# A recurrent attention with a squared-ReLU MLP: new engine orders, half-size operations in the first two steps

## Chip, cores, metric

One core of a Trainium2 chip. The time is device microseconds of one execution, the median of several runs; lower is better. "Span" is the time from the first to the last instruction in the profiled execution.

## What is computed

Four batches, eight heads, 768 positions, 48 channels a head. A decayed outer-product state runs along the positions; its readings, laid side by side over the heads (384 columns), go through a two-layer MLP with a squared ReLU.

```python
# r, k, v, w: (4, 8, 768, 48) f32; u: (8, 48)
for t in range(S):
    cur = einsum('bhd,bhe->bhde', u[None] * kt, vt)
    y[:, :, t] = einsum('bhd,bhde->bhe', rt, state + cur)
    state = wt[:, :, :, None] * state + einsum('bhd,bhe->bhde', kt, vt)
x = y.transpose(0, 2, 1, 3).reshape(3072, 384)
h = x @ w_in                      # w_in (384, 2048)
out = maximum(h, 0) ** 2 @ w_out  # w_out (2048, 384), out (3072, 384) f32
```

## The kernel before

The 3072 rows are cut into 12 **steps** of 256 positions (three a batch). A step lies on 128 partitions, two neighbouring positions (j) a partition, and consists of two chunks (c) of 128 positions. The words below are the names of the operations; `x.s` is the operation x of step s.

*Attention of a step.* `ld.s.w/r/k/v` load 384 KB each through the DMA queue of SP. `ww`, `lw` multiply neighbouring decays and take the log; `cum` sums the logs by matmuls into the PSUM pair `att`; `exp` and `ac` turn the sums into decays. `rw`, `kw` scale one neighbour of r and of k; `rd.s.0` (r) and `rd.s.1` (k) multiply by the decays into `rdec`. These are transposed, by TensorE (`tr`, copied out by `rkt`) in steps 0 to 2 and by DMA (`dtr`) from step 3. `p` multiplies k against r, `pm` masks the product, `su` sums k against v, `ts` and `sn` carry the state S to the next chunk. `ku`, `qp`, `q`, `vq` make the share of u. `y`, `yq`, `yc` add three products up in one PSUM pair, `ysb` copies them out as bf16, `yt` and `xt` (steps 0 to 3) or `dyt` (DMA, later steps) transpose them to `xT`.

*MLP of a step.* Eight `m1.s.g` (six matmuls each) make 2048 hidden columns; `rl.s.g` applies the ReLU and `sq.s.q` squares two groups. In steps 0 to 4 `m2.s.c.q` (four matmuls) multiplies by w_out, and `os` scales. In steps 5 to 11 seven products of halves (`pw.s.1` to `.7`) with sums of halves (`sw`, `tw`) take the place of the eight, put together by `cx` and `ow`. `store` writes 128 rows. w_in and w_out come in four loads each (`ld.g.i`, `ld.g.o`, 768 KB, staging buffers `w_st`) and are cast to f16 (`cast.i.g`, `cast.o.g`). m1 groups 0 and 1 need cast.i.0, 2 and 3 cast.i.1, 4 and 5 cast.i.2, 6 and 7 cast.i.3.

*Order.* The string ORDER is the program: its words are issued one after the other, and each engine works off its own words strictly in this order, waiting for what a word needs. `=A`, `=V`, `=G` put a word on ScalarE (ACT), VectorE (DVE) or GpSimd (POOL); `:n` names the PSUM bank (`one[0..3]`, or pair `att[0..1]`; m, n are pairs of single banks). So the order on an engine and the choice of engine are both written in this string. `warm_.n.i` issues n matmuls on zeros.

*Buffers* go round in lists: `buf(kind, key)` counts the uses of a buffer, given in advance, and puts it back after the last. A load into a buffer waits on SP until it is free, and everything behind it on SP waits too.

Of the kernel before, what the change touches and what calls it, by code (L numbers as in the profile page):

```python
# [22 lines left out]
pm_.1.1 cast.i.1=A yt_.0:3 sn_.0.1 su_.1:0 xt_.0=V qp_.1 ts_.1.0=V m1_.0.1:3 cast.i.2=A pm_.1.0 m1_.0.3:2 m1_.0.0:0  # L23
rl_.0.1=A sn_.1.0 q_.1 ld.2.v cast.i.3=A m1_.0.2:1 rl_.0.3=V m1_.0.4:3 vq_.1 ld.0.o ts_.1.1=V rl_.0.2=A y_.1:1
rl_.0.0=V yc_.1 ld.3.k ww_.2=G yq_.1 m1_.0.5:2 ysb_.1=V ku_.2 m1_.0.6:0 lw_.2 rl_.0.4=V rl_.0.5=A yt_.1:1 sq_.0.0=A
cum_.2:1 ld.1.o xt_.1=V m1_.0.7:3 ld.3.w kw_.2=G rl_.0.6=A m1_.1.1:1 ld.2.o exp_.2 sn_.1.1 m1_.1.4:2 rl_.1.1=V
rl_.0.7=A m1_.1.0:0 rw_.2=G sq_.0.3=A rl_.1.4=V m1_.1.5:1 rl_.1.0=V qp_.2 m1_.1.7:2 rd_.2.0 rl_.1.5=A m1_.1.6:0 ld.3.r
rl_.1.7=A rd_.2.1 tr_.2.0:3 cast.o.0=G rl_.1.6=A m1_.1.2:1 ld.3.o rkt_.2.0=V v_.2=A tr_.2.1:2 rl_.1.2=A m1_.1.3:0
ku_.3 rkt_.2.1=V ac_.2 sq_.1.0=A su_.2:0 q_.2 m2_.0.0.0:1 ld.4.w m2_.0.1.0:3 ts_.2.0=V sq_.0.1=A cast.o.1=G rl_.1.3=V
ld.3.v p_.2.0:1 p_.2.1:0 ww_.3=V sq_.1.1=A m2_.1.1.0:0 vq_.2 m2_.1.0.0:2 pm_.2.1 lw_.3 sq_.1.2=A m2_.0.0.1 pm_.2.0  # L30
# [649 lines left out]
```

## Time and profile before

| | |
|---|---|
| time, median of 3 runs | 178.31 us (177.84 to 179.43) |
| span of the profiled execution | 176.7 us (its whole time is not given; the median lies 1.6 us above the span) |
| PE (matmul) busy | 168.7 us, 95% of the span |
| DVE, ACT, POOL busy | 141.4, 135.7, 125.8 us |
| HBM read, written | 25.17 MB, 4.72 MB |

Busy times are sums over one engine; PE is the matmul row of TensorE, PEld its weight loads, which lie beside it. In a list of instructions the columns are start, duration, engine, source line, operation, output and inputs, shapes, count, and in brackets the idle time before it with what ended that time. Matmul durations include the way through the array, so groups of few matmuls look longer than the distance to the next group. L517 is m1, L540 m2, L594 pw, L454 the y products, L408 p, L430 su, L383 tr, L500 yt, L336 to L340 cum, L238 the spreading of u, L622 the warm-ups.

### The profile page before, as it was taken

The numbers are of one execution on the slowest core, as the hardware profiler recorded it, in microseconds if no ns is written. First come the engines' busy times: TensorE is split into PE (matmuls) and PEld (weight loads), VectorE is DVE, ScalarE is ACT, GpSimd is POOL, SyncE is SP. The second block draws the span as 40 slices with busy tenths as digits, with TensorE's granted clock in tenths as the row PEclk, the third lists the DMA queues.
The fourth block names the chain that finished last, engine by engine and source line by source line (L and its number), as shares of the span: only waits on it lengthen the run. The fifth ranks groups of instructions, "written<-read, shape, count | busy, mean of one in ns | idle before, by whom it ended". The sixth has DMA issues, their size and how long they took to land.

```text
span 176.7 us, 5829 instructions
## 1 busy us (share of the span) xinstructions
PE 168.7 (95%) x2431; PEld 133.3 (75%) x2431; DVE 141.4 (80%) x221; ACT 135.7 (77%) x229; POOL 125.8 (71%) x116
## 2 busy tenths in 40 slices
PE   7969799999999999999999999999999999999993
PEld 2336678866687677578776888889988888989992
DVE  5299976994888968997877979979899879788731
ACT  5677799998659896939899799997897688477320
POOL 6298979999978099969999319759939665165220
DMA  5999999999699999797999959989959930330123
GB/s 142 315 305 340 380 244 347 370 347 254 152 220 240 287 199 254 184 215 179 308 225 194 329 136 222 224 113 269 251 115 132 227 53 4 108 114 4 45 93 134
DMA packets 82667, 36.55 MB, mean 207 GB/s; under 512 B 75857, under 2 KB 81106, under 8 KB 82642
## 3 DMA queue, kind: packets, MB, share of 16 engines
q1 hardware_dynamic: 82642, 36.19, 82.7%
q8 instruction: 19, 0.31, 0.7%
q14 instruction: 6, 0.05, 0.1%
HBM read 25.17 MB, written 4.72 MB: 169 GB/s over the span
## 4 chain that ended last, share of the span: by engine, by line
PE 85%; SPq 6%; DMA 5%; issue 1%; ACT 1%; ACTq 0%
PE one L517 35%; PE one L594 19%; PE one L540 15%; PE att L454 7%; DMA w_st_b<-in_moe_w_in_dram 5%; SPq L205 4%; PE att L408 3%; PE att L430 2%; SPq L213 2%; PE att L338 1%; SPq L233 1%; PE one L500 1%; PE att L340 1%; PE one L383 1%; PE att L336 0%
## 5 line engine op out<-in xcount | busy, mean ns | idle before, releaser
L517 PE MATMUL one<-xT_b,wi_sb 128*128 128x256 bf16 x576 | 70.3, 273 | 0.6 <-ACT gt_b L524 0.4
L517 PEld LDWEIGHTS <-wi_sb 128*128 128x128 f16 x576 | 54.7, 98 | 9.4 <-issue 1.3
L524 ACT ACTIVATE gt_b<-one 128x512 f16<-128x512 f32 x70 | 40.8, 596 | 10.1 <-PE one L517 9.4
L532 ACT ACTIVATE gt_b<-gt_b 128x1024 bf16<-128x1024 f16 x42 | 43.5, 1056 | 1.4 <-DVE gt_b L526 1.0
L419 DVE TENSOR_TENSOR pmT_b<-att,mask 128x1024 bf16<-128x1024 f32 x22 | 26.3, 1217 | 4.2 <-PE att L408 4.2
L540 PE MATMUL one<-wo_sb,gt_b 128*128 128x384 f16 x160 | 28.7, 326 | 0.0
L594 PEld LDWEIGHTS <-gt_b 128*128 128x128 bf16 x280 | 23.2, 98 | 0.9 <-issue 0.4
L311 POOL TENSOR_TENSOR ku_b<-k_b,u_bc 128x768 f32<-128x768 f32 x12 | 22.3, 1862 | 1.0 <-ACT ac_buf L360 0.8
L316 POOL TENSOR_TENSOR ku_b<-ku_b,r_b 128x768 f32<-128x768 f32 x12 | 22.2, 1848 | 0.6 <-DMA r_b<-in_r_dram 0.4
L540 PEld LDWEIGHTS <-gt_b 128*128 128x128 bf16 x160 | 15.1, 98 | 9.6 <-issue 0.5
L444 POOL TENSOR_TENSOR S_b<-t_b,ac_buf 128x384 bf16<-128x384 f32 x20 | 16.9, 846 | 5.4 <-ACT t_b L438 4.8
L526 DVE TENSOR_SCALAR gt_b<-one 128x512 f16<-128x512 f32 x26 | 17.6, 686 | 3.0 <-PE one L517 2.2
L322 POOL TENSOR_TENSOR vq_b<-v_b,q_b 128x768 bf16<-128x768 f32 x12 | 18.2, 1518 | 0.9 <-DVE q_b L319 0.8
L594 PE MATMUL one<-wo_sb,gt_b 128*128 128x192 f16 x168 | 16.2, 246 | 0.0
L374 DVE TENSOR_TENSOR rdec_buf<-r_b,att 128x768 bf16<-128x768 f32 x12 | 11.4, 948 | 1.8 <-POOL r_b L304 0.8
L374 DVE TENSOR_TENSOR rdec_buf<-k_b,att 128x768 bf16<-128x768 f32 x12 | 11.4, 948 | 1.7 <-ACT ac_buf L360 1.1
L319 DVE TENSOR_REDUCE q_b<-ku_b 128x16 f32<-128x768 f32 x12 | 11.3, 944 | 1.7 <-POOL ku_b L316 1.7
L599 ACT ACTIVATE w_st_b<-one 128x192 f32<-128x192 f32 x14 | 4.4, 329 | 10.3 <-PE one L594 10.2
L304 POOL TENSOR_TENSOR r_b<-r_b,w_b 128x384 f32<-128x384 f32 x8 | 8.1, 1014 | 4.7 <-DMA r_b<-in_r_dram 4.7
L292 POOL TENSOR_TENSOR ww_b<-w_b 128x384 f32<-128x384 f32 x7 | 8.0, 1149 | 4.5 <-DMA w_b<-in_w_dram 4.5
L594 PE MATMUL one<-w_st_b,gt_b 128*128 128x192 f16 x112 | 11.2, 246 | 0.0
L440 DVE TENSOR_TENSOR t_b<-S_b,att 128x384 f32<-128x384 bf16 x16 | 8.8, 548 | 2.9 <-POOL S_b L444 2.8
(100 smaller groups left out, 266.5 us busy)
## 6 DMA issues: line engine op xcount, KB each, us to landing
w_b<-in_w_dram SPq DMA_DIRECT2D x12, 384.0 KB, 5.9
r_b<-in_r_dram SPq DMA_DIRECT2D x12, 384.0 KB, 5.4
k_b<-in_k_dram SPq DMA_DIRECT2D x12, 384.0 KB, 5.3
v_b<-in_v_dram SPq DMA_DIRECT2D x12, 384.0 KB, 5.0
out_dram<-w_st_b SPq DMA_DIRECT2D x23, 192.0 KB, 2.2
w_st_b<-in_moe_w_in_dram SPq DMA_DIRECT2D x4, 768.0 KB, 9.5
w_st_b<-in_moe_w_out_dram SPq DMA_DIRECT2D x4, 768.0 KB, 9.1
rkT_b<-rdec_buf SPq DMA_TRANSPOSE x18, 3.5
```

What stands on the lines that cost most here:

```text
L311: nc.gpsimd.tensor_mul(buf("ku", s)[:], buf("k", s)[:, :, 1:3, :], u_bc[:, :, None, :].to_broadcast([C, H, 2, D]))
L316: nc.gpsimd.tensor_mul(ku[:], ku[:], buf("r", s)[:, :, 0:2, :])
L322: nc.gpsimd.tensor_mul(buf("vq", s)[:].rearrange("p j h d -> p h j d"), buf("v", s)[:], buf("q", s)[:, :, :, None].to_broadcast([C, H, 2, D]))
L374: nc.vector.tensor_mul(rdec[:, i, :, heads, 0:D], x.rearrange("p h j d -> p j h d"), decay[:, None, :, :].to_broadcast([C, 2, n, D]))
L419: nc.vector.tensor_mul(pmT, ps_p[:].rearrange("p e (a x) -> p (e a) x", a=2), mk.to_broadcast([C, 4, 2 * C]))
L444: nc.gpsimd.tensor_mul(buf("S", s + c, 1 - c)[:], buf("t", s, c)[:].rearrange("p (a e d) -> p a e d", a=HP, e=2), tiles["a_c", s][:, :, c, ...
L517: nc.tensor.matmul(ps1[:, j, :], wi_sb[:, n // 4, kk, n % 4 * 128:(n % 4 + 1) * 128], xT[:, :, kk, :], start=(kk == 0), stop=(kk == KT - 1))
L524: nc.scalar.activation(rl, m1, AF.Relu, scale=RS)
L526: nc.vector.tensor_scalar(out=rl, in0=m1, scalar1=RS, scalar2=0.0, op0=ALU.mult, op1=ALU.max)
L532: nc.scalar.activation(gt, rl, AF.Square)
L540: nc.tensor.matmul(m2, gt[:, n, c * C:(c + 1) * C], wo_sb[:, n, :], start=(n == 0), stop=(n == NT - 1))
L594: nc.tensor.matmul(where_to, gt[:, n, :], wo[:, n, :], start=(n == 0 and i in (1, 2, 5)), stop=(n == NT // 2 - 1), skip_group_check=True)
```

## The change

All words of ORDER are arranged anew: their order, their engines and their banks. The words are the same but for steps 0 and 1, where

- `rd`, `tr` and `rkt` come in two halves of four heads (`rd_.0.1.0`: step 0, k, heads 0 to 3), which the kernel could do already,
- `ysb`, `yt` and `xt` come in two halves of one chunk (`ysb_.0.1`), which is new code.

`ku`, `qp`, `vq` and `sn` can now go to DVE as well. The accumulation of y may begin with any of `y`, `yq`, `yc`. The uses of `y_sb` and `xT` are counted from ORDER.

The loads begin (SP's words in order) with w, u, k, r, v of step 0, then w, v, r, k of step 1, w_in parts 3 and 0, w of step 2, w_in parts 2 and 1, k and r of step 2, w_out parts 0 and 1. Before: w of 0 and 1, u, r and k of 0, k and r of 1, v of 0, w_in part 0, v of 1, w_in parts 1, 2 and 3, w, k, r, v of 2, w_out part 0.

Words by engine, before and after: `ku`, `qp` on DVE 0 and 0, now 3 and 3 (POOL 12 and 12, now 9 and 9); `vq` on DVE 0, now 2; `sn` on DVE 0, now 2; `cast` ACT 6, POOL 2, now ACT 3, DVE 3, POOL 2; `rl` ACT 70, DVE 26, now 67 and 29; `sq` ACT 42, DVE 6, now 40 and 8; `sw` DVE 40, POOL 16, now 32 and 24; `cx` ACT 16, DVE 5, now 11 and 10; `xt` DVE 4, now ACT 6; `ysb` ACT 8, DVE 4, now ACT 12, DVE 2. Warm-ups: before, 10 ahead of `cum.0`, then 1, 4, 4, 1 and 4 among the work of steps 0 and 1; now 1, 1, 4 and 4 ahead of `ub` and `cum.0`, and 4 and 10 between `cum.0` and the first `tr`. The single one at the end stays.

The diff, ORDER cut to the first lines and the last ones:

```diff
 ORDER = """
-ld.0.w warm_.10.1 ld.1.w ld.0.u ld.0.r ld.0.k ld.1.k ww_.0=V lw_.0 ld.1.r cum_.0:1 ww_.1=V ub_:1 lw_.1 exp_.0 ld.0.v
-rw_.0=G ac_.0 warm_.1.3 uc_=A cum_.1:0 ld.0.i kw_.0=V warm_.4.3 ku_.0 ac_.1 rd_.0.0 exp_.1 ld.1.v rd_.0.1 tr_.0.0:0
-rkt_.0.0=A kw_.1=V ld.1.i tr_.0.1:1 rw_.1=G rd_.1.1 warm_.4.2 ld.2.i rkt_.0.1=A ld.3.i qp_.0 warm_.1.0 rd_.1.0 v_.0=A
-ld.2.w p_.0.0:n pm_.0.0 su_.0:1 tr_.1.1:2 ts_.0.0=A q_.0 p_.0.1:0 rkt_.1.1=A sn_.0.0 warm_.4.0 pm_.0.1 ld.2.k
-cast.i.0=A vq_.0 tr_.1.0:3 rkt_.1.0=V y_.0:0 v_.1=A ku_.1 ts_.0.1=V yc_.0 yq_.0 ld.2.r p_.1.1:n ysb_.0=A p_.1.0:1
...
+warm_.1.3 warm_.1.0 ld.0.w warm_.4.2 ld.0.u ld.0.k ld.0.r warm_.4.3 ld.0.v ww_.0=V ld.1.w lw_.0 ub_:1 cum_.0:1 uc_=A
+kw_.0=V warm_.4.0 exp_.0 ld.1.v warm_.10.1 ac_.0 ku_.0=V rd_.0.1.0 tr_.0.1.0:2 rw_.0=G ld.1.r rd_.0.1.1 qp_.0=G
+rd_.0.0.1 v_.0=A tr_.0.0.1:3 tr_.0.1.1:1 rd_.0.0.0 ld.1.k rkt_.0.1.1=A rkt_.0.0.1=V su_.0:1 rkt_.0.1.0=V p_.0.1:0
+ww_.1=G q_.0 ts_.0.0=A tr_.0.0.0:1 ld.3.i pm_.0.1 sn_.0.0=G ld.0.i rkt_.0.0.0=A lw_.1 ld.2.w vq_.0=G v_.1=A ts_.0.1=V
+p_.0.0:m yc_.0:0 pm_.0.0 cum_.1:1 ld.2.i sn_.0.1=G yq_.0 ac_.1 ld.1.i rw_.1=V exp_.1 y_.0 kw_.1=V ysb_.0.0=A rd_.1.0.0
+ysb_.0.1=A yt_.0.0:0 ku_.1=G yt_.0.1:1 tr_.1.0.0:3 xt_.0.1=A rd_.1.1.0 rd_.1.1.1 tr_.1.1.0:2 xt_.0.0=A qp_.1=G
+rkt_.1.0.0=V su_.1:0 cast.i.3=A rd_.1.0.1 rkt_.1.1.0=V tr_.1.1.1:0 tr_.1.0.1:3 ld.2.k ts_.1.0=V p_.1.0:1 q_.1
+sn_.1.0=G m1_.0.7:2 rkt_.1.1.1=A pm_.1.0 ld.2.r rkt_.1.0.1=A cast.i.0=A vq_.1=G p_.1.1:n m1_.0.6:3 pm_.1.1 yc_.1:1
+rl_.0.6=A ww_.2=G yq_.1 rl_.0.7=A m1_.0.1:3 lw_.2 y_.1 rl_.0.1=A ld.0.o sq_.0.3=V ts_.1.1=V m1_.0.0:2 ysb_.1.1=A
+cast.i.2=V cum_.2:0 ld.1.o ysb_.1.0=A yt_.1.1:0 yt_.1.0:3 xt_.1.0=A rl_.0.0=V m1_.0.5:1 xt_.1.1=A exp_.2 ac_.2
+sq_.0.0=V m1_.0.4:2 rl_.0.5=V m1_.1.0:0 cast.i.1=G rl_.0.4=A m1_.1.1:3 rl_.1.0=A m1_.1.7:1 ku_.2=G kw_.2=V rl_.1.1=A
+ld.2.v ld.3.w m1_.0.2:0 rl_.1.7=V m1_.1.6:3 rd_.2.1 m1_.1.2:2 rw_.2=G rl_.1.6=A sq_.1.0=A m1_.1.3:1 rl_.0.2=V qp_.2=G
+rd_.2.0 rl_.1.2=A m1_.0.3:3 ld.2.o tr_.2.1:0 rl_.1.3=V rl_.0.3=A tr_.2.0:2 rkt_.2.1=V cast.o.0=G m1_.1.4:1 rkt_.2.0=V
+m1_.1.5:3 ld.3.o q_.2 sn_.1.1=G p_.2.0:0 sq_.1.1=A ld.3.k rl_.1.4=A p_.2.1:1 cast.o.1=V m2_.1.0.0:2 sq_.0.2=A v_.2=A
+rl_.1.5=A m2_.0.1.0:1 ww_.3=G sq_.0.1=V pm_.2.1 ld.4.w m2_.1.0.1 m2_.1.1.0:0 pm_.2.0 m2_.0.1.1 m2_.0.0.0:3 vq_.2=V
+lw_.3 sq_.1.2=A su_.2:0 ld.3.r sq_.1.3=A y_.2:1 cast.o.2=V yq_.2 m2_.0.0.1 ts_.2.0=V m2_.0.1.2 sn_.2.0=G cum_.3:0
...
+store.8.1 pw_.11.7 pw_.10.3 ow_.11.4=V ow_.10.4=V pw_.11.3 store.11.1.1 ow_.10.2=V store.10.0 pw_.10.4 ow_.11.2=V
+store.11.0 pw_.11.4 ow_.10.3=A store.10.1 warm_.1.5 ow_.11.3=A store.11.1.0
 """
...
-    def product(name, s):
-        return nc.gpsimd.tensor_mul if where[name, s] == "G" else nc.vector.tensor_mul
+    def product(*word):
+        return nc.vector.tensor_mul if where[word] == "V" else nc.gpsimd.tensor_mul
...
     def ku_(s):
-        nc.gpsimd.tensor_mul(buf("ku", s)[:], buf("k", s)[:, :, 1:3, :],
+        product("ku_", s)(buf("ku", s)[:], buf("k", s)[:, :, 1:3, :],
...
     def y_mm(s, c, cols, lhsT, rhs, j=None):
+        if ("y", s) not in tiles:
+            tiles["y", s] = att[next(int(slot[n, s]) for n in ("y_", "yc_", "yq_") if (n, s) in slot)]
...
+    def ysb_(s, c=None):
+        ps_y, y_sb = tiles["y", s][:, :, 0:DM], buf("y_sb", s)[:]
+        copy = nc.scalar.copy if where[("ysb_", s) + (() if c is None else (c,))] == "A" else nc.vector.tensor_copy
...
+        elif c is None:
+            copy(y_sb, ps_y)
+        else:
+            copy(y_sb[:, c, :], ps_y[:, c, :])
```

More of the change, by code (lines that the diff above doesn't have):

```diff
@@ new lines @@
+su_.6:0 rl_.4.7=V rl_.4.6=A m1_.4.5:3 rd_.7.0 ts_.6.0=A m1_.4.3:1 store.0.0 rl_.4.5=A kw_.7=G dyt_.5 m1_.4.2:0
+sn_.6.0=G rd_.7.1 m2_.4.0.0:3 ld.7.v ku_.7=G os_.3.1=A ts_.6.1=V dtr_.7.0 p_.6.1:1 rl_.4.3=A p_.6.0:0 pm_.6.1
+sq_.4.2=A rl_.4.2=A m1_.5.2:1 qp_.7=G pm_.6.0 m1_.5.6:2 rl_.5.2=A m1_.5.3:0 ld.8.k rl_.5.6=A ld.8.w m1_.5.1:1 v_.7=A
+sn_.6.1=G rl_.5.3=V rl_.5.1=A tw_.3=V sq_.5.1=A yc_.6:0 yq_.6 ld.8.r y_.6 sq_.4.1=A store.2.1 su_.7:1 ysb_.6=V
+m1_.5.5:0 ku_.8=V q_.7 m1_.5.0:2 m2_.4.0.1 dyt_.6 sq_.4.3=A m2_.4.0.2 rl_.5.0=A ww_.8=V m2_.4.0.3 kw_.8=V m1_.5.4:1
@@ new lines @@
+ts_.7.0=V ld.8.v lw_.8 rl_.5.5=A rw_.8=G cum_.8:0 os_.4.0=A store.4.0 sn_.7.0=G ni_.8=V dtr_.7.1 qp_.8=G ts_.7.1=V
+sq_.5.0=A m1_.5.7:2 m2_.4.1.0:0 m2_.4.1.1 rl_.5.4=V m2_.4.1.2 m1_.6.1:3 m2_.4.1.3 m1_.6.6:1 ac_.8 exp_.8 rd_.8.1
+ld.9.w v_.8=A rd_.8.0 rl_.5.7=A ld.10.w ld.11.w sq_.5.2=A os_.4.1=V sw_.5.0.1=G vq_.7=G p_.7.1:1 p_.7.0:0 ld.9.k
+pm_.7.1 rl_.6.1=A ld.9.r m1_.6.2:2 sn_.7.1=G rl_.6.6=A m1_.6.4:1 sq_.5.3=A ww_.9=G m1_.6.0:0 rl_.6.2=A yq_.7:1 pm_.7.0
+sw_.5.1.1=G q_.8 yc_.7 rl_.6.0=A rl_.6.4=A y_.7 sw_.5.0.2=V su_.8:0 m1_.6.3:2 m1_.6.5:1 pw_.5.1:3 sw_.5.1.2=V
@@ new lines @@
+rl_.11.2=V sw_.9.1.1=G m1_.11.7:3 m1_.10.1:1 rl_.10.1=V m1_.11.4:0 rl_.11.7=A sq_.10.1=A m1_.11.3:2 rl_.11.4=A
+sw_.9.1.3=G pw_.9.2:1 sq_.10.0=A rl_.11.3=V pw_.9.1:0 sw_.9.0.2=V sw_.9.1.2=V sw_.10.0.1=G m1_.11.1:3 m1_.11.5:2
+cx_.9.1=A sq_.11.3=A ow_.9.1=V sw_.9.1.4=G pw_.9.6 rl_.11.5=A pw_.9.5 sq_.11.2=A sw_.10.1.3=V rl_.11.1=V cx_.9.2=V
+pw_.10.1:2 sq_.11.0=V cx_.9.3=V sw_.9.0.4=V pw_.9.7 sw_.11.1.1=V sq_.11.1=A cx_.10.1=A pw_.10.2:3 sw_.11.1.3=G
+ow_.9.4=V pw_.9.3 sw_.10.0.2=V ow_.10.1=V pw_.9.4 ow_.9.2=V store.9.0 pw_.10.6 sw_.11.1.2=V ow_.9.3=V pw_.11.2:1
@@ L167 @@
                 if word.startswith("store.") and word.count(".") == 3}
+    counted = dict(y_sb=("ysb_", "yt_", "dyt_"), xT=("xt_", "dyt_", "m1_"))
     def uses_of(kind, key):
+        if kind in counted:
+            return sum(word.partition(".")[0] in counted[kind] and
+                       int(word.partition("=")[0].partition(":")[0].split(".")[1]) == key[0] for word in ORDER.split())
         if kind == "S":
@@ L315, in qp_ @@
         ku = buf("ku", s)
-        nc.gpsimd.tensor_mul(ku[:], ku[:], buf("r", s)[:, :, 0:2, :])
+        product("qp_", s)(ku[:], ku[:], buf("r", s)[:, :, 0:2, :])
     def q_(s):
@@ L321, in vq_ @@
     def vq_(s):
-        nc.gpsimd.tensor_mul(buf("vq", s)[:].rearrange("p j h d -> p h j d"), buf("v", s)[:],
+        product("vq_", s)(buf("vq", s)[:].rearrange("p j h d -> p h j d"), buf("v", s)[:],
                              buf("q", s)[:, :, :, None].to_broadcast([C, H, 2, D]))
@@ L442, in sn_ @@
     def sn_(s, c):
-        nc.gpsimd.tensor_mul(buf("S", s + c, 1 - c)[:],
+        product("sn_", s, c)(buf("S", s + c, 1 - c)[:],
                              buf("t", s, c)[:].rearrange("p (a e d) -> p a e d", a=HP, e=2),
@@ L459, in y_ @@
     def y_(s):
-        tiles["y", s] = att[int(slot["y_", s])]
         pmT, v_bf = buf("pmT", s), buf("v_bf", s)
```

138 lines of the change are left out of this document (55 added, 83 removed).

## The prediction

> **What bounds the kernel now.** I read the page first, then the busy time of the engines by stretches, then the chain that ended last, then the first 30 us instruction by instruction. The page:
>
> ```profile
> span 176.7 us, 5829 instructions
> PE 168.7 (95%) x2431; PEld 133.3 (75%) x2431; DVE 141.4 (80%) x221; ACT 135.7 (77%) x229; POOL 125.8 (71%) x116
> ```
>
> TensorE (PE) is busy 95% of the span. A mean hides where the other 5% lies, so the stretches come next (columns: stretch, length, PE, PEld, DVE, ACT, POOL busy, granted clock, DMA share, GB/s):
>
> ```profile
> 15.00:20.00 5.00, 3.82 (x111) 2.92 (x110) 4.43 (x8) 4.20 (x5) 4.96 (x5) 1.00 1.04 375
> 25.00:30.00 5.00, 5.00 (x57) 4.28 (x53) 3.18 (x5) 4.63 (x8) 4.83 (x5) 1.00 1.01 308
> 35.00:40.00 5.00, 5.00 (x61) 2.99 (x59) 4.90 (x7) 4.76 (x7) 4.47 (x5) 1.00 1.08 347
> ```
>
> From 25 us on PE is full. What can be won lies in the first 25 us, where DVE, ACT, POOL and the DMA engines are all nearly full too, and in the tail. The chain that ended last says the same:
>
> ```profile
> 11.76 9.50 DMA w_st_b<-in_moe_w_in_dram
> ...
> 36.19 0.57 PE att L408 x32
> 36.76 4.01 PE one L540 x24
> 40.77 1.25 PE att L454 x52
> ...
> 153.12 6.55 PE one L517 x60
> 159.67 13.88 PE one L594 x168
> ...
> 173.62 0.33 ACT w_st_b L599
> ```
>
> A load of w_in stands on the chain at 11.76 us. Behind it the chain is PE alone until 173.55 us, then one copy, one store and the end: 3.1 us of tail. One m1 word (six matmuls) is 6.55/10 = 0.655 us of PE, one m2 word 4.01/6 = 0.67 us.
>
> **The change, part by part.** PE gets the same matmuls: 576 of m1, 160 of m2, the same products of halves, the same transposes in smaller groups. So the time changes by three terms only: when PE gets its dense work, new waits of PE in the middle, and the tail. The tail has the same last words in the same order (last pw.11.4, ow.11.3 on ACT, the half store), so I take 0 for it.
>
> *Start.* Rows of the first 28 us (start, duration, engine, line):
>
> ```profile
> 1.19 4.17 PE L622 MATMUL one<-warm 128*128 128x512 bf16 x10 [1.19 <-DVE warm L260]
> 6.06 0.91 PE L238 MATMUL one<-u_row,ones_row 1*128 1x384 f32 x2
> 6.59 0.79 ACT L353 ACTIVATE att<-att 128x768 f32<-128x768 f32 x1
> 6.84 1.00 POOL L304 TENSOR_TENSOR r_b<-r_b,w_b 128x384 f32<-128x384 f32 x1 [3.00 <-DMA r_b<-in_r_dram]
> 7.55 1.02 PE L622 MATMUL one<-warm 128*128 128x512 bf16 x4
> 8.54 0.56 DVE L308 TENSOR_TENSOR k_b<-k_b,w_b 128x384 f32<-128x384 f32 x1 [2.47 <-DMA k_b<-in_k_dram]
> 8.65 2.12 POOL L311 TENSOR_TENSOR ku_b<-k_b,u_bc 128x768 f32<-128x768 f32 x1 [0.81 <-ACT ac_buf L360]
> 9.01 0.95 DVE L374 TENSOR_TENSOR rdec_buf<-r_b,att 128x768 bf16<-128x768 f32 x1
> 9.88 0.95 DVE L374 TENSOR_TENSOR rdec_buf<-k_b,att 128x768 bf16<-128x768 f32 x1
> 10.02 0.62 PE L383 MATMUL one<-ident,rdec_buf 128*128 128x128 bf16 x8 [1.44 <-DVE rdec_buf L374]
> ...
> 25.31 1.48 PE L517 MATMUL one<-xT_b,wi_sb 128*128 128x256 bf16 x12
> 26.63 0.50 PE L500 MATMUL one<-ident,y_sb_b 128*128 128x128 bf16 x6
> 27.39 4.75 PE L517 MATMUL one<-xT_b,wi_sb 128*128 128x256 bf16 x42
> ```
>
> Today k of step 0 is awaited until 8.54 us. In the new queue it goes third instead of fifth, so kw.0 can run some 2 us sooner. Does that help? On PE the u row (ub, 0.84 us until PE's next matmul) now stands ahead of cum.0, behind ten warm-ups that end at 5.36 us as before. So cum.0 ends near 6.9 us and exp.0 near 7.7 us, 0.3 us later than today (6.59 + 0.79). Then 14 warm-ups stand between cum.0 and the first transposes, at 0.21 to 0.26 us each (1.02/4): PE is not free before 9.9 us (10.5 at the upper price). DVE has by then done kw.0, ku.0 and the four half rd. So the half transposes come at 10.0, as the full ones do today: **the early load of k is spent on warm-ups and on ku.0**. What stays is that r and k arrive together.
>
> From there DVE is the chain. Its prices by operation and shape (busy, mean ns):
>
> ```profile
> L526 DVE TENSOR_SCALAR gt_b<-one 128x512 f16<-128x512 f32 x26 | 17.6, 686 | 3.0 <-PE one L517 2.2 <-ACT gt_b L524 0.6
> L374 DVE TENSOR_TENSOR rdec_buf<-r_b,att 128x768 bf16<-128x768 f32 x12 | 11.4, 948 | 1.8 <-POOL r_b L304 0.8 <-POOL vq_b L322 0.6 <-ACT att L353 0.4
> L388 DVE COPY rkT_b<-one 128x1024 bf16<-128x1024 bf16 x3 | 2.1, 688 | 0.4 <-PE one L383 0.4
> L319 DVE TENSOR_REDUCE q_b<-ku_b 128x16 f32<-128x768 f32 x12 | 11.3, 944 | 1.7 <-POOL ku_b L316 1.7
> L419 DVE TENSOR_TENSOR pmT_b<-att,mask 128x1024 bf16<-128x1024 f32 x22 | 26.3, 1217 | 4.2 <-PE att L408 4.2
> L416 DVE TENSOR_TENSOR pmT_b<-one,mask 128x512 bf16<-128x512 f32 x4 | 2.6, 686 | 0.4 <-PE one L408 0.4
> L440 DVE TENSOR_TENSOR t_b<-S_b,att 128x384 f32<-128x384 bf16 x16 | 8.8, 548 | 2.9 <-POOL S_b L444 2.8
> L534 DVE TENSOR_TENSOR gt_b<-gt_b 128x1024 bf16<-128x1024 f16 x6 | 4.7, 787 | 0.0
> L559 DVE TENSOR_TENSOR w_st_b<-wo_sb 128x1536 f16<-128x1536 f16 x2 | 2.1, 1035 | 0.0
> L304 DVE TENSOR_TENSOR r_b<-r_b,w_b 128x384 f32<-128x384 f32 x4 | 3.8, 955 | 0.1
> L572 DVE TENSOR_TENSOR gt_b<-gt_b 128x512 bf16<-128x512 bf16 x11 | 5.5, 511 | 0.0
> ```
>
> Behind each other two 0.95 us operations start 0.87 us apart (9.01, 9.88), so I take 0.08 off each. From 768 and 512 elements (0.948, 0.686) follows about 0.16 us fixed and 1.02 ns an element: a half rd is 0.55, spaced 0.47; a half rkt about 0.42, spaced 0.34. A half costs more than half.
>
> The queue that DVE must work off from rkt.0.0.1 (10.5 us) to the end of cast.i.2, in order: 2 rkt 0.7, q.0 0.87, pm.0.1 1.14, ts.0.1 0.47, pm.0.0 (two banks) 1.3, rw.1 and kw.1 0.95 (by the 0.56 row), 3 rd 1.4, rkt 0.34, rd 0.47, rkt 0.34, ts.1.0 0.47, q.1 0.87, pm.1.0 1.14, pm.1.1 1.3, sq.0.3 0.71, ts.1.1 0.47: 12.9 us. Then cast.i.2 on DVE, which no row shows (DVE copying 1536 f32 of SBUF): from below 0.95 by L559 (1536 elements of 16 bit), from above 1.75 by L526's rate. I take 1.3. Following PE, ACT and POOL alongside I find some 0.4 us in which DVE waits for them (xt.0.0 frees the bank of tr.1.1.1; rl.0.7 stands behind cast.i.0 on ACT). So m1.0.5, which waits for cast.i.2, starts at **T = 10.5 + 12.9 + 0.4 + 1.3 = 25.1 us**; with all lower prices 24.2, with all upper ones and slower warm-ups 26.5.
>
> The Trainium skill ("VectorE: DVE Perf Modes", Mode 2×_2P) says that a one-source copy within SBUF moves two f32 a cycle; by it the cast would be near the lower end and T 24.8. No row here shows it.
>
> What T is worth: ahead of m1.0.5 the new order has on PE all that the old one has done by 25.31 us, and besides it the transposes of y of step 1 and cum.2 (26.63 to 27.39: 0.76 us), but one m1 less (0.655). So the new order is even with the old one at T = 25.41 us. **First term: 25.1 - 25.4 = -0.3 us (-1.2 to +1.1).** The four casts of w_in, the halves and the loads give no more than that, because DVE's queue replaces the DMA on the chain.
>
> Dead covers: cast.i.1 goes to POOL behind ww.2 and is due only at m1.0.2, some 3 us later; with w of step 2 ahead of the last two w_in loads these land one step load later, which that cover hides.
>
> *Middle.* DVE is given 3 ku, 3 qp, 2 vq (128x768 f32) and 3 casts, and rid of 8 sw (0.51 each); the other moves (rl, sq, cx, os on; ww, xt, ysb off) about cancel. A 768 product on DVE: twice the 0.56 of kw alone less the fixed part, 0.95, or twice the 0.955 of L304, 1.9; I take 1.3, nearer the free case. Together +7 to +16 us on 141.4: DVE at 84 to 89%, in stretches where it has 4.90 of 5 already. The tightest place is step 2. From the start of tr.2.0 to m2.0.1.2 PE has 0.45 + 2 m1 1.31 + p 0.57 + 7 m2 4.65 + su 0.45 + y and yq 0.8 = 8.2 us. DVE, from rkt.2.1 to cast.o.2, on which that m2 waits: 2 rkt 1.2, q.2 0.87, cast.o.1 1.3, sq.0.1 0.71, 2 pm 2.3, vq.2 1.3, cast.o.2 1.3 = 9.0 us. **Second term: +0.8 us** (0 with the lower prices; 2.1 with the upper ones). Behind cast.o.2 stand ts.2.0, kw.3 and ysb.2, so the state of step 2 comes late by the same, once.
>
> Sum on the profiled execution: 176.7 - 0.3 + 0.8 = 177.2 us of span. The median of 178.31 lies 1.6 us above that span; the same change on it gives **178.8 us**.
>
> **Rivals.** *The start really shrinks* (0.18). If the 14 warm-ups end by 9.3 us, halves cost half, the cast 0.9 and nothing waits, T is near 23.2, and the middle stays full: 178.3 - 2.2 = 176.1, or 175.6 with one more wait gone. For: the chain loses whole-step waits for r and k. Against: DVE's queue above adds up to 12.9 without a wait.
>
> *DVE stretched by POOL* (0.28; the one on the other side). A product of one and the same shape took DVE 0.56 us at 8.54, when POOL had just been idle, and 0.955 in the mean of L304, later and beside a busy POOL. Eight products more on DVE beside a POOL that is 71% busy go to 1.9 each; ku.0 waits for rw.0 (T + 0.6) and vq.2, qp.3 and the casts lie in the queue above: +2.1 in step 2, and some more at ku.8, ku.9, qp.9, qp.10. From a mean of 1.6 us for these products on, DVE's queue is longer than PE's everywhere it is tight. 178.3 + 0.3 + 2.5 = 181.1. The Trainium skill ("SBUF — State Buffer", SBUF: two separate sides) goes further: a DVE operation with two SBUF inputs and a POOL operation exclude each other, the loser blocks wholly. By it each could wait a POOL operation of 1 to 1.8 us; the 0.4 us of the L304 row is far less than that in the mean.
>
> *PE slows down* (0.06). The first ten warm-ups took 0.42 each, the later ones 0.26, with nothing but activity between. The new order has no warm-ups from 10 to 19 us, where PE is half idle. Did it drop to the slow pace once more for as long as the first ten took (4.17 us), half of that would be lost: 178.8 + 2.1 = 180.9. Against: the idle 1.44 us ahead of the row at 10.02 did not do it. The Trainium skill ("TensorE: Matmul & The Clock Gate", Part 1: The HAM clock gate) asks for an idle window of about 3.4 us, which I don't see coming.
>
> **How the numbers follow.** Forecast (start even, one short wait in step 2) 0.48, 177.0 to 180.0; the three rivals 0.18, 0.28 and 0.06. A measurement of this kernel tells about 1% (176.5 to 180.1) from no change. Faster by over 1%: the first rival, 0.18, and 0.02 of the forecast's own edge; slower: 0.28 + 0.04 of PE's pace + 0.03 of the edge = 0.35; within: 0.45. Range 175.9 to 182.0.
>
> **What would show it.** Right: the first transposes at about 10 us, 14 warm-ups ahead of them; m1.0.5 at 24.2 to 26.5 us behind a DVE cast; DVE above 4.5 of 5 from 10 to 25 us; a wait of PE of about a microsecond between 36 and 43 us; the tail 3 us. Wrong: PE full from 23 us or earlier (then the first term is mis-sized), or several waits of PE beyond 45 us, with DVE products of L311, L316 or L322 near 2 us (then the second rival holds).

## The result and the profile after

| | before | after |
|---|---|---|
| time, median | 178.07 us (177.31 to 179.43, 4 runs) | 185.13 us (183.27 to 187.39, 4 runs) |
| ratio, 95% interval | | 1.037 [1.029, 1.045] |
| profiled execution: span | 176.7 us | 183.2 us (time 184.98 us) |

The change makes the kernel 3.7% slower. The forecast was 178.8 us, and the range ended at 182.0. The ratio, here and below, leaves out executions more than 1.5% above the fastest of the same kernel, so it can differ from the ratio of the medians. The page of after:

```profile
span 183.2 us, 5820 instructions
PE 172.0 (94%) x2430; PEld 135.1 (74%) x2431; DVE 154.8 (85%) x238; ACT 130.7 (71%) x226; POOL 125.3 (68%) x114
PEclk9996599999999999999999999999999999999999
```

PE's share is nearly as before (94% against 95%), so it tells nothing. The line of the granted clock does: in the fourth and fifth slice (13.7 to 22.9 us) it is down. The stretches (length, PE, PEld, DVE, ACT, POOL busy, granted clock, DMA share, GB/s), the first two answering to those shown of before:

```profile
15.00:20.00 5.00, 3.25 (x47) 2.28 (x38) 5.00 (x9) 3.55 (x6) 3.84 (x2) 0.53 1.02 331
25.00:30.00 5.00, 4.18 (x71) 3.55 (x71) 4.90 (x6) 3.96 (x10) 4.47 (x3) 1.00 0.94 306
...
30.00:150.00 120.00, 116.80 (x1737) 91.34 (x1737) 105.86 (x151) 94.30 (x158) 85.91 (x70) 1.00 0.97 213
```

From 15 to 20 us PE did 47 matmuls where it did 111 before, at half the clock, while DVE was busy for the whole 5.00 us. And from 30 to 150 us PE stood idle for 3.2 us (120 - 116.80). Before, that stretch was full:

```profile
30.00:150.00 120.00, 120.00 (x1826) 94.57 (x1824) 103.13 (x148) 100.95 (x171) 94.35 (x76) 1.00 0.93 213
```

What DVE did there shows in the list of instructions of after:

```profile
14.65 2.19 POOL L318 TENSOR_TENSOR ku_b<-k_b,u_bc 128x768 f32<-128x768 f32 x1
15.09 2.16 DVE L315 TENSOR_TENSOR k_b<-k_b,w_b 128x384 f32<-128x384 f32 x1
17.17 0.54 DVE L381 TENSOR_TENSOR rdec_buf<-r_b,att 128x384 bf16<-128x384 f32 x1
17.77 1.07 PE L390 MATMUL one<-ident,rdec_buf 128*128 128x128 bf16 x8 [0.96 <-DVE rdec_buf L381]
...
25.53 1.46 POOL L232 CAST wi_sb<-w_st_b 128x1536 f16<-128x1536 f32 x1 [1.87 <-DMA w_st_b<-in_moe_w_in_dram]
25.74 2.07 DVE L232 CAST wi_sb<-w_st_b 128x1536 f16<-128x1536 f32 x1
26.96 2.52 POOL L318 TENSOR_TENSOR ku_b<-k_b,u_bc 128x768 f32<-128x768 f32 x1
27.87 4.39 PE L529 MATMUL one<-xT_b,wi_sb 128*128 128x256 bf16 x37 [0.82 <-DVE wi_sb L232]
28.51 1.51 DVE L546 TENSOR_TENSOR gt_b<-gt_b 128x1024 bf16<-128x1024 f16 x1
```

kw.1 took 2.16 us, almost four times the 0.56 us of the same product at 8.54 us before. It began 0.44 us after POOL's ku.1 (L318) and ended 0.41 us after it (17.25 against 16.84). cast.i.2 began 0.21 us after POOL's cast.i.1 and ended 0.82 us after it; sq.0.0 ended 0.54 us after ku.2. Each ends about when POOL does plus its own free time (0.56; 0.95 for the two casts of w_out in this profile; 0.69 for sq.0.3 at 24.66 us), less some 0.15 us: **these DVE operations, whose operands all lie in SBUF, started while POOL ran and waited for it**. Before, the same products hardly meet POOL:

```profile
10.74 0.55 DVE L308 TENSOR_TENSOR k_b<-k_b,w_b 128x384 f32<-128x384 f32 x1
11.06 1.09 POOL L304 TENSOR_TENSOR r_b<-r_b,w_b 128x384 f32<-128x384 f32 x1 [0.30 <-DMA r_b<-in_r_dram]
```

There kw.1 starts 0.03 us before ku.0 ends (8.65 + 2.12 = 10.77), and POOL's rw.1 begins only when kw.1 has 0.23 us left. kw.0 at 8.54 began 0.11 us ahead of POOL's ku.0 and was not held up; ku.0 itself took 2.12 us where later ones take 1.8.

So m1.0.5 starts at T = 27.87 us, against the break-even of 25.41: 2.46 of the 6.5 us. The tail is 3.07 us (3.08 before). The other 4.05 us come between T and the tail: the 3.2 us of idle PE, and some 0.85 us that no wait explains.

### The profile page after: what moved, and what is told of

It is laid out like the page before. It is cut to its first block, busy times and chain, and to the rows that moved or that the text cites. A ratio compares the mean times of both kernels' runs of the same rounds, so it can differ in the third digit from the quotient of the medians.

```text
span 183.2 us, 5820 instructions
## 1 busy us (share of the span) xinstructions
PE 172.0 (94%) x2430; PEld 135.1 (74%) x2431; DVE 154.8 (85%) x238; ACT 130.7 (71%) x226; POOL 125.3 (68%) x114
## 4 chain that ended last, share of the span: by engine, by line
PE 66%; DMA 11%; POOL 6%; ACT 5%; DVE 5%; issue 4%; SPq 2%; ACTq 0%; POOLq 0%
PE one L529 25%; PE one L606 15%; PE one L552 9%; DMA xT_b<-y_sb_b 5%; PE att L463 4%; PE one L634 4%; DMA v_b<-in_v_dram 3%; DMA out_dram<-w_st_b 3%; PE att L437 2%; POOL ku_b L323 2%; PE att L415 2%; PE one L390 2%; ACT gt_b L536 2%; DVE wi_sb L232 1%; SPq L398 1%
## 5 line engine op out<-in xcount | busy, mean ns | idle before, releaser
L536 ACT ACTIVATE gt_b<-one 128x512 f16<-128x512 f32 x67 | 38.7, 596 | 13.4 <-PE one L529 12.4
L544 ACT ACTIVATE gt_b<-gt_b 128x1024 bf16<-128x1024 f16 x40 | 41.4, 1053 | 0.4 <-DVE gt_b L538 0.2
L538 DVE TENSOR_SCALAR gt_b<-one 128x512 f16<-128x512 f32 x29 | 19.7, 685 | 3.8 <-PE one L529 3.7
L552 PEld LDWEIGHTS <-gt_b 128*128 128x128 bf16 x160 | 15.1, 98 | 9.3 <-issue 0.2
L318 POOL TENSOR_TENSOR ku_b<-k_b,u_bc 128x768 f32<-128x768 f32 x9 | 18.6, 2065 | 0.0
L323 POOL TENSOR_TENSOR ku_b<-ku_b,r_b 128x768 f32<-128x768 f32 x9 | 17.1, 1905 | 0.2
L329 POOL TENSOR_TENSOR vq_b<-v_b,q_b 128x768 bf16<-128x768 f32 x10 | 15.1, 1512 | 3.2 <-PE one L529 3.2
L381 DVE TENSOR_TENSOR rdec_buf<-k_b,att 128x768 bf16<-128x768 f32 (+1 forms) x14 | 11.5, 833 | 1.6 <-ACT att L360 0.8
L360 ACT ACTIVATE att<-att 128x768 f32<-128x768 f32 x12 | 9.6, 802 | 3.4 <-PE att L347 3.0
L381 DVE TENSOR_TENSOR rdec_buf<-r_b,att 128x768 bf16<-128x768 f32 (+1 forms) x14 | 11.6, 833 | 0.5 <-POOL k_b L315 0.4
L584 POOL TENSOR_TENSOR gt_b<-gt_b 128x512 bf16<-128x512 bf16 x6 | 7.6, 1271 | 3.9 <-DVE sg_b L584 3.8
```

The costliest lines, as they stand in the source:

```text
L318: product("ku_", s)(buf("ku", s)[:], buf("k", s)[:, :, 1:3, :], u_bc[:, :, None, :].to_broadcast([C, H, 2, D]))
L323: product("qp_", s)(ku[:], ku[:], buf("r", s)[:, :, 0:2, :])
L329: product("vq_", s)(buf("vq", s)[:].rearrange("p j h d -> p h j d"), buf("v", s)[:], buf("q", s)[:, :, :, None].to_broadcast([C, H, 2, D]))
L381: nc.vector.tensor_mul(rdec[:, i, :, heads, 0:D], x.rearrange("p h j d -> p j h d"), decay[:, None, :, :].to_broadcast([C, 2, n, D]))
L536: nc.scalar.activation(rl, m1, AF.Relu, scale=RS)
L538: nc.vector.tensor_scalar(out=rl, in0=m1, scalar1=RS, scalar2=0.0, op0=ALU.mult, op1=ALU.max)
```

## The experiments

Two theories for the start: **port** (DVE blocked behind POOL, kw.1 above all) and **clock** (PE at half pace from 15 to 22 us). For the rest: **late loads** (loads and transposing DMAs late in SP's queue). Before ran at 177.4 to 177.7 us beside these runs.

**One half of the order alone.** The new words up to `sn_.1.1` with before's behind them, and before's words up to `rkt_.2.1` with the new ones behind.

> The words of the changed kernel up to sn_.1.1 (the steps 0 and 1 and the start of step 2), then all other words in the order, on the engines and in the banks of before. Theory (the loss has two parts: the start costs 2.5 us, because the last dense stretch of PE begins at 27.87 instead of the 25.4 us of equality, and the waits of PE from 85 to 130 us cost some 3.2 us): 178.1 + 2.5 = 180.6 us, PE without waits after 40 us. Rival (the start alone carries the loss, since all later queues run behind it): 184 to 185 us. Rival (the start is harmless, the rest of the order carries it): 178 us.

> The mirror: the words of before up to rkt_.2.1, then all others as in the changed kernel. Theory of two parts: 178.1 + 3.2 to 4.0 = 181.3 to 182.1 us, PE dense from 25.3 us as before, and waits of PE between 85 and 130 us again (ahead of cum.8, p.9, su.9 and m1.8, 2.9 us in the changed kernel). Rival (start alone): 178 us. Rival (rest alone): 184 to 185 us.

Measured: 185.33 us (1.043 [1.037, 1.049]) and 182.74 us (1.030 [1.025, 1.035]). Each half costs, and both cost more than expected; together they cost more than the whole. Part of the first is its seam, the place where the words of one order follow those of the other. There PE waits for v of step 2:

```profile
PE att L436 <- ACT v_bf_b L306: 1.4, 1, 1.4
```

Behind that seam before's words run as they did before, so a late start alone does no harm to the middle. Another part belongs to this execution: ub took 1.64 us there (0.91 in after), the first transposes came at 11.98 instead of 9.65 us, and T is 30.49 instead of 27.87. In the half with the new rest PE waits for copies of v, as it did in after at 119.83 us:

```profile
PE att L434 <- ACT v_bf_b L304: 1.2, 2, 0.9
```

**kw.1 on POOL**, a single word of after:

```diff
-kw_.1=V
+kw_.1=G
```

> The changed kernel with one word on another engine: kw_.1 goes from DVE to POOL, where it stands ahead of ku_.1. Theory (a DVE product of two SBUF operands that begins beside a POOL operation waits until that one ends: kw.1 took 2.16 us beside ku.1 of 14.65 to 16.84, where the same shape alone takes 0.56): rd of step 1 begins at about 15.8 instead of 17.17 us, the cast before m1.0.5 ends 1 us or more earlier, and the time falls by 1 us or more if the later cast does not meet a POOL operation again. Rival (2.16 us is the price of kw on DVE in this place whatever POOL does, or POOL's longer queue gives it all back): rd of step 1 no earlier than 17 us or m1.0.5 at 27.9 us as now, time unchanged within 0.5 us.

Measured: 180.90 us (1.019 [1.014, 1.023]). One word takes 4.2 us off the median; by the two ratios, each against its own runs of before, it is 1.8 points or some 3.2 us.

```profile
14.98 1.38 POOL L315 TENSOR_TENSOR k_b<-k_b,w_b 128x384 f32<-128x384 f32 x1
15.73 0.55 DVE L381 TENSOR_TENSOR rdec_buf<-r_b,att 128x384 bf16<-128x384 f32 x1 [0.23 <-ACT att L360]
...
24.47 0.95 DVE L232 CAST wi_sb<-w_st_b 128x1536 f16<-128x1536 f32 x1
25.64 2.56 PE L529 MATMUL one<-xT_b,wi_sb 128*128 128x256 bf16 x22
```

The first rd of step 1 starts 1.44 us sooner (15.73 against 17.17), the cast meets no POOL operation and takes 0.95 us, and T is 25.64. That the cast ran free was luck: cast.i.1 came on POOL only at 26.40 us in this execution, when its load landed (25.53 in after; see the run with v sooner).

**Warm-ups among the work of steps 0 and 1**, ten matmuls in three places, kw.1 still on DVE:

```diff
 tr_.0.0.0:1
+warm_.2.3
...
 y_.0
+warm_.3.2
...
 yt_.0.1:1
+warm_.5.2
```

> The changed kernel with ten more warm-ups in the gaps of PE between 12 and 18 us: 2 behind tr_.0.0.0, 3 behind y_.0, 5 behind yt_.0.1. Rival to the port (PE's clock: the granted clock is 0.53 from 15 to 20 and 0.79 from 20 to 25 us): the clock stays at 1.00, su, tr, p and m1 between 15.9 and 22.4 us take their usual time, the dense stretch begins 1.5 to 2 us earlier, and the time falls by as much. Theory of the port: the clock stays at 1.00, but the start of dense work still hangs on DVE (kw.1 and the cast), so it moves by less than 0.5 us and the time by less than 1 us.

Measured: 181.79 us (1.021 [1.016, 1.026]). This was a miss for the port theory, which gave the clock less than 1 us.

```profile
15.50 2.17 DVE L315 TENSOR_TENSOR k_b<-k_b,w_b 128x384 f32<-128x384 f32 x1
```

```profile
15.00:20.00 5.00, 4.75 (x72) 2.43 (x65) 5.00 (x9) 3.96 (x7) 4.26 (x3) 1.00 1.03 354
```

kw.1 is blocked as in after, the clock stays at 1.00, and T is 26.88. From the start of kw.1 to the start of cast.i.2 it takes 9.46 us here (15.50 to 24.96) and 10.65 in after (15.09 to 25.74), so the slow PE costs some 1.2 us on this chain and is a cause beside the port. That it makes up the whole gain, 3.3 us by the medians and 2.8 by the ratios, is not shown: two executions of after with a mean granted clock of 0.981 and 0.991 took 183.27 and 185.29 us, the one with more slow time being the shorter.

**Both together.**

> The changed kernel with both mendings of the start: kw_.1 on POOL and the ten more warm-ups between 12 and 18 us. Each alone took 3 to 4 us off 185.1 (180.9 and 181.8). Theory (both act on the same chain of DVE and PE between 15 and 28 us, so they add up only in part, and what is left against before lies in the waits behind 85 us): 179.5 to 180.5 us, clock 1.00 from 15 to 25 us, dense work of PE from about 25 us. Rival (two independent losses): 177.5 us.

Measured: 180.99 us (179.75 to 186.82; 1.017 [1.011, 1.023]): no better than kw.1 alone, and above the 179.5 to 180.5 expected. The profiled execution, of 186.82 us, shows one way in which the new start varies:

```profile
5.57 1.64 PE L245 MATMUL one<-u_row,ones_row 1*128 1x384 f32 x2
...
7.86 5.86 PE L634 MATMUL one<-warm 128*128 128x512 bf16 x14
13.56 0.61 PE L390 MATMUL one<-ident,rdec_buf 128*128 128x128 bf16 x8
```

PE was still at its first, slow pace there: ub took 1.64 us (0.91 before), the 14 warm-ups 0.42 each, and the first transposes came at 13.56 instead of 9.65 us. (The column of the granted clock reads 1.00 in these first microseconds, so this pace is read from the durations.) In the eight profiles that begin with the words of after, ub took 0.91 (three times), 0.96, 1.03, 1.10 and 1.64 us (twice): the pace rises sooner or later from run to run, and the new order puts ub and 14 warm-ups just where that shows.

**On top of both, ub and uc behind cum.0 and fewer warm-ups** (six between the first transposes in place of ten ahead of them):

```diff
-ub_:1 cum_.0:1 uc_=A kw_.0=V warm_.4.0 exp_.0 ld.1.v warm_.10.1 ac_.0 ku_.0=V rd_.0.1.0
+cum_.0:1 ub_:1 exp_.0 uc_=A kw_.0=V warm_.4.0 ld.1.v ac_.0 rd_.0.1.0
...
+tr_.0.1.1:1 warm_.6.0 ku_.0=V
```

> As e5_kw1_warm, and the spreading of u (ub, two f32 matmuls) behind cum_.0 instead of ahead of it, ku_.0 on DVE behind the two rd of k, ten warm-ups fewer there but six between the transposes. Theory (where PE's clock rises late, as in the profile of e1, the f32 matmuls run at the slow pace ahead of cum.0 and everything behind them is 1 to 1.4 us later; with ub behind cum.0 exp.0 no longer hangs on it): exp.0 ends by 7.2 us instead of 7.6 to 8.9, time 0.5 to 1.5 us below e5. Rival (the first chain is set by the landing of r of step 0 at 7.7 us and by DVE anyway): equal to e5 within 0.5 us.

Measured: 182.63 us (1.029 [1.023, 1.035]), a miss. The first transposes came at 8.28 us, but T was 25.98: rw.1 began on DVE at 15.14 us, no sooner than with kw.1 alone (14.96). DVE was busy for 4.76 of 5 us from 10 to 15 us and waited there for no load of step 1. Why it is slower than the run without this edit stays open.

**That start with before's words behind it.**

> The start of e6 up to sn_.1.1, all other words as before the change. Theory (start and rest lose separately; the mended start is about even with the old one): 177.0 to 178.5 us, no wait of PE behind 45 us. Rival (the new start is worse by itself even when mended, its DVE being full to 35 us): 180 us or more.

Measured: 184.41 us (1.039 [1.035, 1.043]), another miss, and no proof against the start: PE waits 4.2 us in three places at and behind the seam, and T is 26.80, since cast.i.2 met cast.i.1 again (1.76 us).

```profile
PE one L552 <- POOL wo_sb L232: 1.6, 1, 1.6
PE att L437 <- ACT v_bf_b L307: 1.4, 1, 1.4
PE att L463 <- POOL vq_b L329: 1.2, 1, 1.2
```

**The loads of v sooner**, in the half with the new rest, and then in after with kw.1 on POOL:

```diff
 ld.7.r
+ld.7.v
...
 ld.8.v
+ld.9.v
```

> As e2_rest_new (start of before, rest of the changed kernel, 182.7 us), with two loads moved up in SP's queue: v of step 9 ahead of w of steps 9 to 11, v of step 7 ahead of the transposes of step 6. Theory (the waits of PE ahead of su.7 and su.9, and behind them those on the DMA transposes of y, come from v landing late behind transposes and stores in SP's queue): su.7 and su.9 don't wait, PE's waits from 85 to 130 us fall from 1.6 us to 0.5 or less, and the time falls by 1 to 2 us. Rival (ACT and DVE are late there anyway): the same sum of waits in other places, time within 0.7 us of e2.

> The new kernel with kw.1 on POOL and with the loads of v of steps 7 and 9 up in SP's queue (9 behind v of step 8, 7 behind r of step 7). If the loss is the blocked product at the start (worth 4.2 us in the earlier run) and the late loads (worth 2.2 us where they were moved alone), the two add: 178.4 to 179.4 us, first dense m1 near 25.7, no wait of PE on v later. If late waits only move to the next late buffer: as with kw.1 alone, 180.5 to 181.5.

Measured: 180.49 us (1.018 [1.011, 1.025]) and 181.72 us (1.022 [1.013, 1.030]). The first is 2.25 us below the run that it mends, a little more than expected, but its profile does not bear the reason out: its m1 work began 2.3 us sooner (19.14 against 21.45), with ub at 0.91 us against 1.64: the pace rose sooner in that run. PE's idle time from 60 to 150 us is 1.8 us in both. There the waits on v (1.2 us) are gone, and two on transposing DMAs have come:

```profile
PE one L527 <- DMA xT_b<-y_sb_b: 0.9, 1, 0.9
PE att L413 <- DMA rkT_b<-rdec_buf: 0.5, 1, 0.5
```

The second missed 178.4 to 179.4. Its waits, where those with kw.1 alone were 0.2 and 0.5 us and none on v:

```profile
PE att L415 <- DMA rkT_b<-rdec_buf: 2.1, 2, 1.6
PE one L529 <- DMA xT_b<-y_sb_b: 0.5, 1, 0.5
```

The transposing DMAs that now stand behind the loads in SP's queue come late. **The wait moved along the queue.** Its T missed too, 26.85 where 25.7 was expected, although its words are those of the run with kw.1 alone up to step 6:

```profile
24.25 1.73 POOL L232 CAST wi_sb<-w_st_b 128x1536 f16<-128x1536 f32 x1 [1.06 <-DMA w_st_b<-in_moe_w_in_dram]
25.04 1.75 DVE L232 CAST wi_sb<-w_st_b 128x1536 f16<-128x1536 f32 x1
```

Here the load of w_in part 1 landed 2.15 us sooner, POOL began cast.i.1 at once, and cast.i.2 started inside it and took 1.75 us instead of 0.95. It also started 0.57 us later (25.04 against 24.47), with the granted clock at 0.53 from 15 to 20 us against 0.66.

**Before without its 14 warm-ups after the first ten.**

> The old kernel without its 14 warm-up matmuls that stand between the first ten and 19 us (it keeps the first ten). If small gaps of PE alone bring its clock down: granted clock below 0.9 in one of the stretches from 5 to 20 us and 1 to 3 us more, 179 to 181. If an idle 1.5 us does not bring it down, as the prediction held: 1.00 from 10 us on and no change, 177.2 to 178.2.

Measured: 178.69 us (1.0047 [1.0012, 1.0082]).

```profile
10.00:15.00 5.00, 3.65 (x66) 2.82 (x67) 4.50 (x7) 3.60 (x5) 3.82 (x5) 0.61 1.10 365
15.00:20.00 5.00, 4.54 (x98) 3.62 (x100) 3.70 (x6) 4.40 (x5) 5.00 (x4) 0.50 1.04 393
20.00:25.00 5.00, 5.00 (x88) 4.09 (x84) 4.64 (x7) 4.25 (x5) 3.16 (x4) 0.87 0.96 262
```

The clock falls as the clock theory says, for some ten microseconds, and costs 0.2 to 1.5 us by the interval, at or below the lower end of the 1 to 3 us expected with it. A slow PE was cheap here, where DVE or a load set the pace.

**One part of the change on before: all loads of step 0 first** (u, k, r, v of step 0 ahead of w and k of step 1), **and the halves of r, k and y alone** (y in halves in step 0 only).

> The old kernel with one part of the change alone: u, k, r and v of step 0 ahead of every load of step 1. If the loads themselves are harmless and the loss lies in the engines' orders: within 0.5 us of before, 177.2 to 178.4. If later loads of step 1 starve the start: DVE waits on w or k of step 1, 1 to 3 us more.

> The old kernel with the other part alone: r and k of steps 0 and 1 multiplied, transposed and copied in halves of the heads, y of step 0 copied and transposed in halves of the chunks; engines as before. By the prices of the prediction a half costs more than half: 4 rd more at 0.08 us on DVE, 3 or 4 copies more on ACT at about 0.1 to 0.16: 0 to +1.0 us, 177.7 to 178.7. If the halves in fact shorten the start: 176.5 to 177.5.

Measured: 182.56 us (1.027 [1.018, 1.035]) and 178.07 us (1.001 [0.998, 1.004]). The halves cost nothing that can be measured (0.4% at most). The loads alone cost 2.7%, more than the 1 to 3 us expected, since before's order has DVE work on w of step 1 second:

```profile
DVE ww_b L296 <- DMA w_b<-in_w_dram: 5.7, 2, 5.1
```

PE's granted clock was down there as well (0.50 from 10 to 15 us). The new order avoids that wait by putting ww.1 on POOL and all products of step 1 behind step 0. There kw.1 and ku.1 both come up, at 15 us.

**The whole start mended**: kw.1 on POOL, cast.i.2 on POOL and cast.i.1 on DVE, with the ten warm-ups and without.

```diff
-kw_.1=V
+kw_.1=G
...
-cast.i.2=V
+cast.i.2=G
...
-cast.i.1=G
+cast.i.1=V
```

> The new kernel with the start mended in all three places: kw.1 on POOL; cast.i.2, the cast that the dense work waits for, on POOL and cast.i.1 on DVE in its stead, so that no DVE operation on the chain can be blocked by a POOL cast; and the eight extra warm-up matmuls that hold PE's clock. If the start carries the loss: first dense m1 at or below 25.4 us, granted clock 1.00, 178.0 to 179.5. If the rest of the new order costs its own 1.8% whatever the start does: 180.5 to 181.5, with the first dense m1 just as early.

> The same without the extra warm-ups. If PE's clock is worth about a microsecond here (as in the old kernel without its warm-ups): a granted clock of 0.5 to 0.7 in the stretch from 15 to 20 us and 0.5 to 1.5 us above the run with them. If the clock is the larger part: 2 us or more above it.

Measured: 181.88 us (1.024 [1.012, 1.035]) and 181.02 us (1.019 [1.014, 1.023]). T is 25.45 and 25.56, the clock 1.00 and 0.66 from 15 to 20 us:

```profile
25.45 4.74 PE L529 MATMUL one<-xT_b,wi_sb 128*128 128x256 bf16 x40
```

```profile
30.00:150.00 120.00, 118.69 (x1784) 93.00 (x1784) 108.68 (x157) 95.64 (x159) 88.91 (x72) 1.00 0.96 210
```

The start is even with before, and the kernel is still 2% slower: that is the rest. With kw.1 free, the extra warm-ups bring nothing that can be measured; with kw.1 blocked they brought some 3 us. The profiles together (T; what cast.i.2 took; span less T, 151.3 us in before by the break-even; PE idle from 60 to 150 us):

| | T, us | cast.i.2, us | span - T, us | PE idle 60 to 150, us |
|---|---|---|---|---|
| before | 25.41 (break-even) | | 151.3 | 0.00 |
| before with halves; without warm-ups; loads first | | | | 0.25; 0.00; 0.21 |
| new start, rest of before | 30.49 | 2.10 | 152.8 (seam 1.4) | 0.01 |
| ub later, rest of before | 26.80 | 1.76 | 155.9 (seam 3.0) | 1.2 |
| after | 27.87 | 2.07 | 155.3 | 3.2 |
| kw.1 on POOL | 25.64 | 0.95 | 152.5 | 1.0 |
| warm-ups | 26.88 | 1.86 | 154.4 | 2.3 |
| both | 29.84 | 1.75 | 155.2 | 3.0 |
| kw.1 on POOL, v early | 26.85 | 1.75 | 154.5 | 2.8 |
| ub later | 25.98 | 0.95 | 154.3 | 2.0 |
| start mended, with and without warm-ups | 25.45, 25.56 | on POOL | 153.4, 154.0 | 1.1, 1.8 |
| start of before, new rest; with v early | | | | 1.8, 1.8 |

With before's words behind 60 us PE has next to no wait, even behind the start with the largest T; the one exception is a wait of 1.2 us for POOL's vq at 84 us in the run with ub later. With the new words it has 1 to 3 us in every profile, at waits that change with the start. Whatever is undone at the front, 1 to 3 us come back there.

## Why the prediction was wrong

*First term (start): wrong, by its prices.* The frame held: the first transposes came at 9.65 us behind 14 warm-ups (10.0 predicted), DVE was the chain, m1.0.5 waited for cast.i.2, and with both blocks gone T is 25.5 to 25.6 (25.41 the break-even, 25.1 predicted). What failed is "rw.1 and kw.1 0.95 (by the 0.56 row)": kw.1 took 2.16; and cast.i.2, priced at 1.3 between 0.95 and 1.75, took 2.07, above the upper end. These two terms are short by 1.6 and 0.8 us, 2.4 of the 2.8 us between T = 25.1 and 27.87. Free, it takes 0.95 us, the lower end. The Trainium skill ("VectorE: DVE Perf Modes", Mode 2×_2P) had pointed there, and the trace agrees. A price from an undisturbed row was used for a place where POOL runs. The prediction named cast.i.1 on POOL, but only as a cover with 3 us to spare, and not as what cast.i.2 would wait for.

*Rival "DVE stretched by POOL" (0.28): the right mechanism at the wrong place and size.* The Trainium skill's rule ("SBUF — State Buffer", SBUF: two separate sides: the one that starts first holds the pair for its whole instruction) was set aside because the mean of L304 showed 0.4 us. A mean over four products hides whether one of them starts inside a POOL operation. The trace agrees with the rule: 1.6 us for kw.1, 1.1 us for cast.i.2. But the eight moved products, on which the rival was built, were never held up (DVE groups by shape, busy and mean ns; L315 is kw, with kw.1 among its seven):

```profile
L315 DVE TENSOR_TENSOR k_b<-k_b,w_b 128x384 f32<-128x384 f32 x7 | 5.7, 809 | 1.7 <-DMA k_b<-in_k_dram 1.7
L318 DVE TENSOR_TENSOR ku_b<-k_b,u_bc 128x768 f32<-128x768 f32 x3 | 2.9, 953 | 0.8 <-DMA k_b<-in_k_dram 0.8
L323 DVE TENSOR_TENSOR ku_b<-ku_b,r_b 128x768 f32<-128x768 f32 x3 | 2.8, 949 | 0.0
L329 DVE TENSOR_TENSOR vq_b<-v_b,q_b 128x768 bf16<-128x768 f32 x2 | 1.9, 949 | 0.0
```

The moved ones, L318, L323 and L329, took 0.95 us each, the lower price.

*Rival "PE slows down" (0.06): underrated.* The argument against it, that 1.44 us of idle time did not do it, looked at one gap. In after the granted clock fell between 15.0 and 15.5 us, with no gap of PE above 0.67 us from 9.65 to 15.1 us, after it had been 3.87 of 5 us busy in short pieces. In before, with 4.32 of 5 in that stretch and warm-ups among them, it kept its pace. The share of busy time alone does not decide: before with halves had 3.55 of 5 us from 15 to 20 us and stayed at 1.00. The price, 2.1 us, is of the order of what the warm-ups brought while kw.1 was blocked (some 3 us, of which 1.2 are traced to the clock), and too high otherwise (0.5% in before).

*Second term (step 2): did not happen.* From 30 to 60 us PE is busy for 29.98 of 30 us, because the products took 0.95 and the start was late anyhow. The waits came where the prediction had set nothing, nearly all beyond 95 us (its own sign of being wrong, but without slow products on DVE):

```profile
119.83 0.52 PE L437 MATMUL att<-v_bf_b,rdec_buf 64*128 64x96 bf16 x16 [0.49 <-ACT v_bf_b L307]
127.20 0.83 PE L529 MATMUL one<-xT_b,wi_sb 128*128 128x256 bf16 x6 [1.47 <-DMA xT_b<-y_sb_b]
```

SP's queue of the same run around them:

```profile
111.18 1.32 SPq L398 DMA_TRANSPOSE rkT_b<-rdec_buf  x1
112.55 0.58 SPq L630 DMA_DIRECT2D out_dram<-w_st_b  x1
113.17 0.45 SPq L212 DMA_DIRECT2D v_b<-in_v_dram  x1
...
121.59 1.22 SPq L519 DMA_TRANSPOSE xT_b<-y_sb_b  x1
```

v of step 9 is issued at 113.17 us, behind a transposing DMA and a store in SP's queue, and ACT can copy it only at 118.94 us. On ACT ysb.8 stands behind that copy: PE had ended its y products at 119.33 us, but ysb.8 ran from 120.75 to 121.56, dyt.8 was issued at 121.59, and m1 of step 8 waited for it until 127.20. So one late load has a part in both waits. The failed step here is the second term: the prediction counted engines in the middle and not SP's queue, and put nothing behind step 2, where 3.2 us of PE's time were lost. The tail was as predicted.

*Open:* why the new rest gives PE these waits beyond the queue's order; some 0.2 to 0.85 us of span in the profiles of the new order that no wait of PE explains; how much of the warm-ups' gain is the clock. That DVE and POOL meet differently from run to run is shown for cast.i.2 (0.95 and 1.75 us behind the same words in one pair of runs, 0.95 and 1.76 us in another); that this makes the wider spread of the new order is argued.

## What to carry over

Before moving a two-input product or an f32 cast to DVE, look up what POOL does at that moment, not the product's mean: if it starts inside a POOL operation, it costs about what is left of that operation on top, and a load that lands at another time can decide whether it does. A chain that was bound by a load can be bound by DVE, by POOL or by PE's clock at nearly the same time; here mending either of two causes gave about 3 us or more, and mending both gave no more than one. And an order found as a whole is tight in SP's queue too: in both runs that moved loads up, the transfers behind them came late instead.

## What the runs showed of the hardware

DVE operations with one operand in PSUM were not held up: two rd (L374) ran at 0.95 us each from 9.01 to 10.83 us beside POOL's ku.0, in before. PE's granted clock fell to half (0.50 from 15.5 us in after) and stayed there for 3.41, 6.83 or 10.24 us in each of the seven profiles that show it, multiples of one time (summed over stretches of half a microsecond; 3.41 with kw.1 on POOL, 6.83 in after, 10.24 in before without its later warm-ups). PE's pace first rises at a moment that differs between runs of one start (ub 0.91 to 1.64 us). The Trainium skill ("TensorE: Matmul & The Clock Gate", Part 1: The HAM clock gate) lets the array cool after an idle window of about 3.4 us; in after it cooled while it was busy three quarters of the time, with gaps of 0.67 us at most until then, so the measurement decides. The same page tells of another kernel in which short idle times between groups made the clock swing (A second HAM failure mode), which fits better. That the first rise varies from run to run stands in Part 1 too, and these traces agree.
